# Attention and a two-product feed-forward in one kernel: float64 weight words put together from bytes, and three float32 head pairs scaled before their transposes

## Chip, cores and metric

The kernel runs on one core of a Trainium2 chip (trn2). The metric is the device time of one execution in microseconds, as a median over runs. Instructions run on five engines with queues of their own: TensorE (PE; its weight loads are listed as PEld), VectorE (DVE), ScalarE (ACT), GpSimd (POOL) and SyncE (SP), which here only issues DMAs.

## What is computed

Inputs: q, k and v, float32, 4 batches of 8 heads with 768 positions of 64 numbers; `moe_w_in` (512 x 2048) and `moe_w_out` (2048 x 512), float64.

```python
scores = q @ k.transpose(0, 1, 3, 2) / sqrt(64)
keep = (key < n_sink) | ((0 <= query - key) & (query - key < window))     # 4 sinks, window 128
scores = where(keep, scores, -1e9); scores -= scores.max(-1)
a = exp(scores); a = a / (a.sum(-1) + 1e-9)
x = (a @ v).transpose(0, 2, 1, 3).reshape(3072, 512)
h = x @ w_in
g = where(h >= 1, h, where(h <= -1, 0, (h + 1) ** 2 / 4))
out = g @ w_out
```

## The kernel before

**Chunks and units.** The 3072 tokens are worked on in 8 chunks of 384 (half a batch). A unit is one head of one chunk, so there are 64; chunk 0 needs units 0 to 7, and so on. The first 16 units (two chunks) are computed in float32, as 8 *pairs* of heads (`pair_load`, `pair_scores`, `pair_sums`, `early_transp`, `pair_r`, `pair_av`); the other 48 in split float32r (`load`, `scores`, `transp`, `av`, `sinks`).

**A float32 pair.** `pair_scores(m, i)` makes the scores of query tile i of both heads (TensorE, L441), adds the mask and takes the peak (VectorE, L452), and takes exponentials with their sums (ScalarE, L457). `pair_sums(m)` makes r = 1 / (sum + 1e-9), six numbers per partition (L464, L465). `early_transp` transposes p through PSUM (L474, L476) and ScalarE copies it back (L477 to L480). `pair_r(m)` spreads r over the head's 64 rows with six small products against the identity (L505) and copies the result to `xn` (ScalarE, L507). `pair_av(m)` multiplies the transposed p with v into PSUM (L493), and VectorE multiplies PSUM by what lies in `xn` (L496). Here r acts on the result, behind the products.

**Weights.** Each float64 matrix comes in as 32-bit word pairs. A *weight pair* n (16 of them) is 1 MB: two blocks of `w_in` (n even) or of `w_out` (n odd), 1024 numbers per partition, low and high word side by side, so a stream of high words has a step of 8 bytes. `decode_parts` makes a float32 of each and splits it: L170 shifts the high word left by 3 and masks it, L176 puts the two top bits back, L179 puts in the top three bits of the low word, ScalarE rounds to float32r (L180, `high`), VectorE subtracts (L183, `rest`). The three integer steps go through a tile `bits`. The first four weight pairs are decoded between the steps of the first pairs, in an order written out by hand (`first_pairs`, with `queue`, which chains instructions of one engine); the other twelve are spread among the steps of chunk 0's feed-forward, and each begins with `fetch`, which asks for the raw words of a few later ones. Raw and finished tiles share 8 buffers (`wpool`). The first four loads are issued on SyncE, the others on ScalarE's queue.

**Feed-forward.** Per chunk and per block j of 128 columns: `stage1` (12 matmuls, L588, three float32r products for one float32 one), the function g (L595 to L599), and `stage2` (9 matmuls, L607), two blocks behind. Chunk 0's GpSimd makes the low part `gl`, elsewhere VectorE does.

**What sets the order.** TensorE runs in program order. `spread` merges the steps of the next chunk's attention with those of this chunk's feed-forward by weights that stand beside each step; chunk 0 is merged with pairs 5 to 7, the end of pair 4 and units 16 and 17. On the other engines a scheduler with a timeline of its own sets the order, but for the instructions that are chained by `queue` or held by `keep_in_program_order`.

Of the kernel before, what the change touches and what calls it, by code (L numbers as in the profile page):

```python
# [20 lines left out]
NSINK = 4  # L21
KB = P + NSINK
# [27 lines left out]
def attn_ffn(ctx, tc, qk, qkp, vx, vs, par, w_in, w_out, out):  # L50
    nc = tc.nc
# [31 lines left out]
    low, high = par_f[:, :, 0], par_f[:, :, 1]  # L83
# [37 lines left out]
    behind = nc.gpsimd.memset(m1n[:, P:KB], 0.0).ins  # L121
# [7 lines left out]
    with tc.issue_after(behind):  # L129
# [4 lines left out]
        for r0 in (0, 32, 64, 96):  # L134
            t = tsel2[r0:r0 + R]
# [25 lines left out]
    with tc.issue_after(behind):  # L161
        nc.gpsimd.memset(both, -1)

    def decode_parts(t, w, words, pin=False, on=False):

        low, x = words[..., 0], words[..., 1]
        high, rest = (t[:, :, 0], t[:, :, 1]) if len(t.shape) == 4 else (t[:, 0], t[:, 1])

        def shift():
            first = nc.vector.tensor_scalar(w, x, 3, 0x3FFFFFFF, op0=ALU.logical_shift_left, op1=ALU.bitwise_and)  # L170
            if pin:
                tc.keep_in_program_order(first)
            queue(first, on)

        def sign():
            queue(nc.vector.scalar_tensor_tensor(w, x, -0x40000000, w, op0=ALU.bitwise_and, op1=ALU.bitwise_or), on)  # L176

        def tail():
            queue(nc.vector.scalar_tensor_tensor(w, low, 29, w, op0=ALU.logical_shift_right, op1=ALU.bitwise_or), on)  # L179
            queue(nc.scalar.copy(high, w.bitcast(F32)), on)  # L180

        def rest_of():
            queue(nc.vector.tensor_tensor(rest, w.bitcast(F32), high.bitcast(F32), op=ALU.subtract), on)  # L183

        return shift, sign, tail, rest_of

    def decode(t, w, words, pin=False):
        for f in decode_parts(t, w, words, pin):
            f()
# [4 lines left out]
    def weights(n):  # L194

        def src(k):
            return (w_in, w_out)[k % 2][k // 2 * 2:k // 2 * 2 + 2].bitcast(I32).rearrange("j p c -> p j c")

        def fetch():
            for k in range(n, min(n + min(AHEAD if n > 2 else 1, NP // 2 - n // 2 - 1) + 1, NP)):  # L200
                if k not in raw:
                    raw[k] = wpool.tile([P, 2, 2 * DM], I32, name="w")

                    with tc.issue_after(loaded[-1]) if k < SYNC else nullcontext():
                        (nc.sync if k < SYNC else nc.scalar).dma_start(raw[k], src(k))

        def parts(on):
            j, i = n // 2 * 2, n % 2
            words = raw[n].rearrange("p j (c two) -> p j c two", two=2)
            if i:  # L210
                t = wpool.tile([P, 2, 2, DM], F32R, name="w")
                w_o[j:j + 2] = t[:, 0], t[:, 1]
            else:
                t = wi2[n // 2]
            return decode_parts(t, dec.tile([P, 2, DM], I32, name=f"bits{n % 2}"), words, pin=not on, on=on)

        def f():
# [34 lines left out]
    st = {}  # L252
# [207 lines left out]
    def pair_sums(m):  # L460
        on = m < H // 2
        stat = st.pop(("sum", m))
        r = stat[:, :, CT:2 * CT]
        queue(nc.vector.tensor_scalar(r, stat[:, :, 0:CT], 1.0e-9, None, op0=ALU.add), on)  # L464
        queue(nc.vector.reciprocal(r, r), on)  # L465
        st["r", m] = r

    def early_transp(u, part):

# [12 lines left out]
    def pair_av(m):  # L482

        T = CT * P
        v_s = vq[m % 2]
        ps = ps_a.tile([P, 512], F32, name="ps_a")

        terms = [(2, 4, 1, 2), (0, 0, 2, 0), (1, 2, 2, 1), None]
        for n, t in enumerate(terms):
            for a in range(2):  # L490
                k, s0, ns, i = t or (CT, 0, 1, CT - 1)
                rhs = pt0[a][:, s0 * P:(s0 + ns) * P] if t else spn[a]
                nc.tensor.matmul(ps[a * D:a * D + D, i * P:(i + ns) * P], lhsT=v_s[:, k, a], rhs=rhs,  # L493
                                 start=(n == 0), stop=(n == len(terms) - 1))
        x = xn[:, units[2 * m][1] // 2, :]
        return lambda: queue(nc.vector.tensor_tensor(x, ps[:, :T], x, op=ALU.mult), m < H // 2)  # L496

    def pair_r(m):

        T = CT * P  # L500
        ps = ps_a.tile([P, 512], F32, name="ps_a")
        r = st.pop(("r", m))
        for i in range(CT):
            for a in range(2):
                nc.tensor.matmul(ps[a * D:a * D + D, i * P:(i + 1) * P], lhsT=r[:, a, i:i + 1].broadcast_to([P, D]),  # L505
                                 rhs=ident, start=True, stop=True)
        queue(nc.scalar.copy(xn[:, units[2 * m][1] // 2, :], ps[:, :T]), m < H // 2)  # L507

    def pair_steps(m):

        a, b = 2 * m - 2, 2 * m - 1
        sc = [(0.45, lambda i=i: pair_scores(m, i)) for i in range(CT)] if m < NATIVE // 2 else [(0.0, lambda: None)] * CT
        steps = [(0.0, lambda: pair_load(m + 1))] if m + 1 < NATIVE // 2 else []
        if m < NATIVE // 2:
            steps.append((0.0, lambda: pair_values(m)))
        tp = [(0.35, lambda u=u, i=i: early_transp(u, i)) for u in (a, b) for i in range(2)]
        pv = [(0.65, lambda: pair_r(m - 1)), (1.2, lambda: pair_av(m - 1)())]
        dg = [(0.0, lambda: pair_sums(m))] if m < NATIVE // 2 else []
# [143 lines left out]
    tail = []  # L662
# [159 lines left out]
```

## Time and profile before

| | us |
|---|---|
| median of three runs (705.91 to 710.62) | 706.29 |
| profiled execution | 705.98 |
| its span, from the first to the last instruction | 704.3 |
| TensorE busy in the span | 681.5 |
| VectorE busy | 510.3 |
| ScalarE busy | 489.5 |
| GpSimd busy | 278.8 |

A profile is of one execution. Busy time of TensorE is modelled, since matmuls overlap in its pipeline. A row of a group gives line, engine, operation, output and inputs with their shapes, how many, then busy time and the mean duration, then the engine's idle time just before them with what ended it. [...]

### The profile page before, as it was taken

Reading aid. Unit: us, or ns where it says so; the run is one execution under the profiler, and the core shown is the slowest. Engines: PE = TensorE matmul, PEld = TensorE weight load, DVE = VectorE, ACT = ScalarE, POOL = GpSimd, SP = SyncE. Lnnn points to the kernel's source line nnn. Section 1 sums busy time; section 2 is a strip of 40 time slices with the busy share of each in tenths; the row PEclk is TensorE's granted clock in tenths of the full one; section 3 lists DMA queues with packets and bytes.
Section 4 is the critical chain, followed back from the end, with each engine's and each line's share of the span. In section 5 each row is a group of like instructions: output and inputs, shape, how many; then the busy total and the mean of one; then the engine's idle time right before and its main releaser. Section 6 shows DMA issues by size and latency. Waiting matters only on the chain.

```text
span 704.3 us, 12263 instructions
## 1 busy us (share of the span) xinstructions
PE 681.5 (97%) x3889; PEld 604.6 (86%) x3889; DVE 510.3 (72%) x1405; ACT 489.5 (70%) x1241; POOL 278.8 (40%) x470
## 2 busy tenths in 40 slices
PE   5899998999999999999999999999999999999996
PEld 3567877899999999989889999899899999989995
DVE  7888998887776877688777878878787877642221
ACT  4886667687778868777787877777776876554332
POOL 3003344744443445355554455635544444300000
PEclk9899999999999999999999999999999999999999
DMA  7864533132244344254333443434322310001001
GB/s 232 291 216 156 190 99 135 49 107 60 63 148 124 102 127 129 68 174 128 92 113 105 147 130 124 126 118 133 122 59 62 102 50 22 3 1 45 1 1 49
DMA packets 45441, 73.98 MB, mean 105 GB/s; under 512 B 10744, under 2 KB 30008, under 8 KB 45368
## 3 DMA queue, kind: packets, MB, share of 16 engines
q1 hardware_dynamic: 42104, 60.53, 28.2%
q10 hardware_dynamic: 3264, 12.58, 4.8%
q8 instruction: 33, 0.54, 0.3%
q14 instruction: 40, 0.33, 0.1%
HBM read 66.80 MB, written 6.29 MB: 104 GB/s over the span
## 4 chain that ended last, share of the span: by engine, by line
PE 79%; DVE 9%; DMA 3%; ACT 3%; POOL 3%; issue 2%; SPq 0%; ACTq 0%; POOLq 0%; DVEq 0%
PE h_ps L588 33%; PE o_ps L607 32%; PE ps_a L283 4%; PE ps_a L390 4%; PE ps_a L344 2%; DVE bits L176 2%; DVE bits L179 1%; DMA w<-w_in 1%; POOL q_l L269 1%; PE ps_a L474 1%; DVE w L183 1%; DVE bits L170 1%; PE ps_a L493 1%; DVE p L304 1%; DVE g L597 1%
## 5 line engine op out<-in xcount | busy, mean ns | idle before, releaser
L588 PE MATMUL h_ps<-x,wi 128*128 128x384 f32 x1536 | 310.2, 340 | 0.0
L588 PEld LDWEIGHTS h_ps<-x,wi 128*128 128x128 f32 x1536 | 262.2, 188 | 8.7 <-issue 1.5
L607 PE MATMUL o_ps<-w,gh 128*128 128x512 f32 x768 | 244.0, 398 | 0.0
L607 PE MATMUL o_ps<-w,gl 128*128 128x512 f32 x384 | 151.1, 393 | 0.4 <-POOL gl L599 0.4
L607 PEld LDWEIGHTS o_ps<-w,gh 128*128 128x128 f32 x768 | 134.3, 188 | 16.9 <-issue 1.7
L597 DVE SCALAR_TENSOR_TENSOR g<-g,h_ps 128x384 f32<-128x384 f32 x128 | 70.3, 549 | 61.7 <-ACT g L596 60.6
L595 ACT ACTIVATE g<-h_ps,half 128x384 f32<-128x384 f32 x128 | 73.9, 578 | 52.7 <-PE h_ps L588 52.0
L269 POOL TENSOR_TENSOR q_l<-r,q_h 128x384 fp32r<-128x384 f32 x48 | 51.1, 1064 | 122.7 <-ACT q_h L268 116.1
L598 ACT CAST gh<-g 128x384 fp32r<-128x384 f32 x128 | 65.5, 512 | 46.1 <-DVE g L597 44.9
L290 ACT ACTIVATE p<-p,peak 128x260 f32<-128x260 f32 (+1 forms) x144 | 71.5, 496 | 23.0 <-DVE peak L287 22.4
L607 PEld LDWEIGHTS o_ps<-w,gl 128*128 128x128 f32 x384 | 72.0, 188 | 17.8 <-POOL gl L599 0.7
L599 DVE TENSOR_TENSOR gl<-g,gh 128x384 fp32r<-128x384 f32 x112 | 67.3, 601 | 23.5 <-ACT gh L598 22.6
L267 DVE TENSOR_TENSOR k_s<-k_r,k_s 64x524 fp32r<-64x524 f32 (+1 forms) x44 | 49.1, 1115 | 34.4 <-ACT k_s L265 34.3
L596 ACT ACTIVATE g<-g 128x384 f32<-128x384 f32 x128 | 67.0, 524 | 2.0
L287 DVE CUSTOM_DVE_ANT_0 p<-ps_a,m 128x260 f32<-128x260 f32 (+1 forms) x144 | 57.0, 407 | 14.7 <-PE ps_a L283 13.8
L358 POOL TENSOR_SCALAR_AFFINE_SELECT pt<-pt 128x384 fp32r<-128x384 f32 (+1 forms) x96 | 51.3, 535 | 22.6 <-DVE pt L349 19.5
L304 DVE CUSTOM_DVE_ANT_0 p<-p,stat 128x128 f32<-128x128 f32 x128 | 57.0, 489 | 0.2
L356 POOL TENSOR_SCALAR_AFFINE_SELECT pt<-pt 128x384 fp32r<-128x384 f32 (+1 forms) x96 | 49.9, 521 | 8.8 <-ACT pt L348 4.9
L599 POOL TENSOR_TENSOR gl<-g,gh 128x384 fp32r<-128x384 f32 x16 | 23.4, 1461 | 67.7 <-ACT gh L598 64.2
L390 PEld LDWEIGHTS ps_a<-pt,v_s 128*128 128x128 f32 x304 | 42.4, 190 | 1.8
L390 PE MATMUL ps_a<-pt,v_s 128*128 128x256 f32 (+1 forms) x304 | 41.9, 275 | 0.0
L283 PE MATMUL ps_a<-k_s,q_h 128*128 128x260 f32 (+1 forms) x144 | 40.7, 283 | 1.2 <-DVE sk L352 0.9
(151 smaller groups left out, 933.1 us busy)
## 6 DMA issues: line engine op xcount, KB each, us to landing
r<-qk SPq DMA_DIRECT2D x48, 192.0 KB
k_r<-qk SPq DMA_DIRECT2D x32, 262.0 KB
again<-w_in SPq DMA_DIRECT2D x16, 512.0 KB
again<-w_out SPq DMA_DIRECT2D x16, 512.0 KB
w<-w_in ACTq DMA_DIRECT2D x6, 1024.0 KB
w<-w_out ACTq DMA_DIRECT2D x6, 1024.0 KB
out<-o SPq DMA_DIRECT2D x23, 256.0 KB
r<-vx SPq DMA_DIRECT2D x32, 128.0 KB
```

Source lines behind the costliest of these rows:

```text
L269: nc.gpsimd.tensor_tensor(q_l, q_r, q_h.bitcast(F32), op=ALU.subtract)
L283: nc.tensor.matmul(ps[:, lo:260], lhsT=q[:, i * P:(i + 1) * P], rhs=k_s[:, c0:c0 + 260 - lo], start=(j == 0), stop=(j == len(qs) - 1))
L290: nc.scalar.activation(p[:, i, lo:260], p[:, i, lo:260], AF.Exp, bias=peak_i, scale=-1.0, accum_out=stat[:, i:i + 1])
L304: nc.vector.tensor_tensor_reduce(out=own, in0=own, in1=p[:, i, 0:P], scale=r, scalar=0.0, op0=ALU.add, op1=ALU.add, accum_out=stat[:, i:i ...
L390: nc.tensor.matmul(z, lhsT=w, rhs=y, start=(n == 0), stop=(n == len(mms) - 1))
L588: nc.tensor.matmul(h_ps[:, :T], lhsT=w_i[j][:, w, ct * P:(ct + 1) * P], rhs=x[:, y, ct], start=(ct == 0 and n == 0), stop=(ct == NCT - 1 a ...
L595: nc.scalar.activation(g, h_ps[:, :T], AF.Relu, bias=half, scale=0.5)
L596: nc.scalar.activation(g, g, AF.Square)
L597: nc.vector.scalar_tensor_tensor(g, g, 1.0, h_ps[:, :T], op0=ALU.min, op1=ALU.max)
L598: nc.scalar.copy(gh, g)
L599: (nc.gpsimd if row0 == GL_POOL else nc.vector).tensor_tensor(gl, g, gh.bitcast(F32), op=ALU.subtract)
L607: nc.tensor.matmul(o_ps[tt], lhsT=gg[:, tt * P:(tt + 1) * P], rhs=w_o[j][:, w], start=(j == 0 and n == 0), stop=(j == NJ - 1 and n == 2))
```

## The change

Four things change.

1. A weight word is made in one step from the high word and a tile `ends` (128 x 1024 words, set to 0 once by GpSimd). Two VectorE instructions write single bytes into `ends`: byte 0 of each word gets the top three bits of the low word, byte 3 gets the sign and the bits that turn the exponent. Then `word` shifts the high word left by 3 and takes the xor with `ends`. The result goes over the low words of the raw pair (for the last weight pair into `ends`), so the cast and the subtraction read it from there, with a step of 8 bytes. The tiles `bits` are gone.
2. The raw pair is now in use until the subtraction. `fetch` looks one pair less ahead in places: pair 13 is asked for by step 12 instead of step 11, pair 14 behind the decode of pair 13 instead of ahead of it, pair 15 behind the decode of pair 14.
3. Pairs 5 to 7 (`SCALED`): right behind the sums VectorE multiplies the six tiles of p by r, in place. `pair_r` falls away for them, and `pair_av` ends with a copy by ScalarE instead of VectorE's product.
4. `pair_steps` orders the steps differently: scores and sums of pair m stand ahead of the last transposes of pair m - 1, and the product with v comes last.

The old decode lives on in the code for inputs out of the fast path's range, which isn't run here.

```diff
+SCALED = range(5, NATIVE // 2)
...
+    def decode_parts(t, ends, words, w, on):
+        x = words[..., 1]
+        b = words.bitcast(U8).rearrange("p j c (w e) -> p j c w e", e=4)
+        e = ends.rearrange("p j c -> p (j c)").bitcast(U8).rearrange("p (j c e) -> p j c e", j=2, e=4)
...
+        def put(i):
+            if not on:
+                tc.keep_in_program_order(i)
+            queue(i, on)
...
         def tail():
-            queue(nc.vector.scalar_tensor_tensor(w, low, 29, w, op0=ALU.logical_shift_right, op1=ALU.bitwise_or), on)
+            put(nc.vector.tensor_scalar(e[..., 0], b[..., 0, 3], 5, 0x07, op0=ALU.logical_shift_right,
+                                        op1=ALU.bitwise_and))
         def sign():
-            queue(nc.vector.scalar_tensor_tensor(w, x, -0x40000000, w, op0=ALU.bitwise_and, op1=ALU.bitwise_or), on)
+            put(nc.vector.tensor_scalar(e[..., 3], b[..., 1, 3], 0x80, 0xC0, op0=ALU.bitwise_and, op1=ALU.bitwise_xor))
+        def word():
+            queue(nc.vector.scalar_tensor_tensor(w, x, 3, ends, op0=ALU.logical_shift_left, op1=ALU.bitwise_xor), on)
             queue(nc.scalar.copy(high, w.bitcast(F32)), on)
...
-            for k in range(n, min(n + min(AHEAD if n > 2 else 1, NP // 2 - n // 2 - 1) + 1, NP)):
+            for k in range(n, min(n + min(AHEAD if n > 2 else 1, max(NP // 2 - 1 - (n + 1) // 2, 0)) + 1, NP)):
...
-            return decode_parts(t, dec.tile([P, 2, DM], I32, name=f"bits{n % 2}"), words, pin=not on, on=on)
+            return decode_parts(t, ends, words, ends if n == NP - 1 else words[..., 0], on)
...
+            if NP - 4 < n < NP - 1:
+                wsteps[n + 1].load()
...
+        if m in SCALED:
+            for a in range(2):
+                for i in range(CT):
+                    p = early_p(2 * m + a)[:, i, KB if i == 0 else 0:260]
+                    nc.vector.tensor_scalar(p, p, r[:, a, i:i + 1], None, op0=ALU.mult)
...
+        if m in SCALED:
+            return lambda: nc.scalar.copy(x, ps[:, :T])
...
-        pv = [(0.65, lambda: pair_r(m - 1)), (1.2, lambda: pair_av(m - 1)())]
+        pv = [(1.2, lambda: pair_av(m - 1)())]
+        if m - 1 not in SCALED:
+            pv = [(0.65, lambda: pair_r(m - 1))] + pv
...
-        return steps + tp[:1] + sc[:1] + tp[1:] + sc[1:2] + pv + sc[2:] + dg
+        if m == 5:
+            return steps + tp[:1] + sc[:1] + tp[1:] + sc[1:2] + pv[:1] + sc[2:] + dg + pv[1:]
+        return steps + tp[:1] + sc[:1] + tp[1:2] + sc[1:2] + tp[2:3] + sc[2:] + dg + tp[3:] + pv
```

On VectorE, at the sums of pair 5, in the kernel before (`stat` holds sums and r; `bits_806` is weight pair 7):

```order
L464 TENSOR_SCALAR stat<-stat 128x2x3
L465 RECIPROCAL stat<-stat 128x2x3
L170 TENSOR_SCALAR bits_806<-w 128x1024
L176 SCALAR_TENSOR_TENSOR bits_806<-w,bits_806 128x1024
L597 SCALAR_TENSOR_TENSOR g<-g,h_ps 128x384
L179 SCALAR_TENSOR_TENSOR bits_806<-w,bits_806 128x1024
```

And in the changed one (L188 and L192 write the bytes, L195 the word, L199 subtracts, L488 scales):

```order
L188 TENSOR_SCALAR ends<-w 128x1024
L192 TENSOR_SCALAR ends<-w 128x1024
L199 TENSOR_TENSOR wi_158<-w,wi_158 128x2x512
L479 TENSOR_SCALAR stat<-stat 128x2x3
L195 SCALAR_TENSOR_TENSOR w<-w,ends 128x1024
L480 RECIPROCAL stat<-stat 128x2x3
L488 TENSOR_SCALAR pt<-pt,stat 128x128
L488 TENSOR_SCALAR pt<-pt,stat 128x260 x2
L488 TENSOR_SCALAR pt<-pt,stat 128x128
L488 TENSOR_SCALAR pt<-pt,stat 128x260 x2
L627 SCALAR_TENSOR_TENSOR g<-g,h_ps 128x384
```

A decode has two one-source instructions and one with two sources ahead of its cast, and the bytes of weight pair 7 stand ahead of the subtraction of pair 6; the scaling follows the reciprocal at once. Between the third scores of pairs 5, 6 and 7 and their first transposes, TensorE's order has 18 or 21 `h_ps` matmuls and three to five groups of three `o_ps` matmuls.

On ScalarE, the load of weight pair 14 in the kernel before (`wi6` is the cast of weight pair 12, `w_1200` the raw pair 14; the cast of weight pair 13 comes 13 rows after the first):

```order
L180 CAST wi6_161<-bits0_1139 128x2x512
L205 DMA w_1200<-w_in 128x2x1024
L457 ACTIVATE pt_188,stat_1011<-pt_188,peak_97 128x260
L596 ACTIVATE g_1166<-g_1166 128x384
L480 COPY pt_187<-ps_a_1179 128x384
```

And in the changed one (`w_1139` is the raw pair 13, `w_1197` pair 14):

```order
L196 CAST w_1191<-w_1139 128x2x512
L626 ACTIVATE g_1213<-g_1213 128x384
L501 COPY pt_190<-ps_a_1224 128x256
L502 COPY spn1_180<-ps_a_1224 4x128
L217 DMA w_1197<-w_in 128x2x1024
L628 CAST gh_1214<-g_1213 128x384
```

The load moved from behind the cast of pair 12 to behind that of pair 13 and three more instructions.

On VectorE, where the changed kernel takes up weight pair 14 (the first rows are of pair 13, the second L188 of pair 14):

```order
L188 TENSOR_SCALAR ends<-w 128x1024
L192 TENSOR_SCALAR ends<-w 128x1024
L199 TENSOR_TENSOR wi_161<-w,wi_161 128x2x512
L195 SCALAR_TENSOR_TENSOR w<-w,ends 128x1024
L199 TENSOR_TENSOR w<-w 128x2x512
L627 SCALAR_TENSOR_TENSOR g<-g,h_ps 128x384 x2
L188 TENSOR_SCALAR ends<-w 128x1024
L192 TENSOR_SCALAR ends<-w 128x1024
L302 ISA p,peak<-ps_a,m_109 128x128
```

The same place before (`bits_1203` is weight pair 13, `bits_1271` pair 14):

```order
L179 SCALAR_TENSOR_TENSOR bits_1203<-w,bits_1203 128x1024
L597 SCALAR_TENSOR_TENSOR g<-g,h_ps 128x384
L183 TENSOR_TENSOR w<-bits_1203,w 128x2x512
L496 TENSOR_TENSOR xn<-ps_a,xn 128x384
L170 TENSOR_SCALAR bits_1271<-w 128x1024
L176 SCALAR_TENSOR_TENSOR bits_1271<-w,bits_1271 128x1024
```

Pair 14 still follows pair 13 closely, while its load now follows pair 13's cast; the first scores of unit 16 (L302, before L287) stand right behind it.

## Rows read from the trace of the kernel before

**Rows 1.** The page's busy time of the engines.

```profile
PE 681.5 (97%) x3889; PEld 604.6 (86%) x3889; DVE 510.3 (72%) x1405; ACT 489.5 (70%) x1241; POOL 278.8 (40%) x470
```

**Rows 2.** Windows by stage: busy time of PE, PEld, DVE, ACT, POOL; clock, DMA.

```profile
12.90:44.70 31.80, 24.69 (x203) 17.10 (x202) 29.36 (x85) 25.49 (x84) 0.91 (x2) 0.89 0.79 264
44.70:123.80 79.10, 76.94 (x472) 61.46 (x471) 70.16 (x120) 52.83 (x134) 30.22 (x22) 1.00 0.43 148
...
136.00:650.00 514.00, 512.84 (x2893) 468.22 (x2892) 379.59 (x1123) 378.14 (x957) 232.88 (x403) 1.00 0.31 96
```

**Rows 3.** Chain of waits by line, 12.9 to 44.7, then 44.7 to 123.8.

```profile
by line: DVE bits L179 10.9%; PE ps_a L474 9.8%; DVE bits L176 7.4%; DVE pt L452 6.8%; ACT wi L180 6.6%; ACT pt L457 6.3%; PE ps_a L493 5.0%; PE h_ps L588 4.5%; DVE bits L170 4.3%; DVE p L452 4.2%; DVE x L619 3.9%; DVE w L183 3.8%; ACT p L4
...
by line: PE h_ps L588 21.8%; PE o_ps L607 13.9%; DVE bits L176 9.5%; DVE bits L179 7.1%; issue 4.8%; DVE w L183 4.4%; DVE wi L183 3.8%; PE ps_a L493 3.7%; DVE bits L170 3.4%; DVE g L597 3.2%; PE ps_a L441 3.0%; PE ps_a L474 2.9%; PE ps_a L5
```

**Rows 4.** Groups of VectorE's instructions, 0 to 140 us.

```profile
L179 DVE SCALAR_TENSOR_TENSOR bits<-w,bits 128x1024 int32<-128x1024 int32 x16 | 22.2, 1389 | 0.2
L176 DVE SCALAR_TENSOR_TENSOR bits<-w,bits 128x1024 int32<-128x1024 int32 x16 | 21.8, 1365 | 0.3
L170 DVE TENSOR_SCALAR bits<-w 128x1024 int32<-128x1024 int32 x16 | 11.4, 711 | 2.9 <-DMA w<-w_in 2.9
L183 DVE TENSOR_TENSOR wi<-bits,wi 128x1024 fp32r<-128x1024 f32 x8 | 10.6, 1326 | 4.4 <-ACT wi L180 4.4
L183 DVE TENSOR_TENSOR w<-bits,w 128x1024 fp32r<-128x1024 f32 x8 | 9.8, 1223 | 2.4 <-ACT w L180 2.4
L597 DVE SCALAR_TENSOR_TENSOR g<-g,h_ps 128x384 f32<-128x384 f32 x16 | 8.7, 544 | 0.0
...
L496 DVE TENSOR_TENSOR xn<-ps_a,xn 128x384 f32<-128x384 f32 x8 | 4.4, 551 | 0.4 <-PE ps_a L493 0.3
```

**Rows 5.** VectorE with a pointer scalar: line L302, then a group.

```profile
L302 DVE TENSOR_SCALAR p<-p,stat x16: 275/283/1049, 122.5 to 267.0; 128x128 f32<-128x128 f32 x16
...
L114 DVE TENSOR_SCALAR m<-x,nw 128x260 f32<-128x260 f32 x1 | 0.3, 350 | 0.0
```

**Rows 6.** Lines L170 and L176: ns min/median/max, first and last start.

```profile
L170 DVE TENSOR_SCALAR bits<-w x16: 650/682/1046, 12.9 to 123.8; 128x1024 int32<-128x1024 int32 x16
L176 DVE SCALAR_TENSOR_TENSOR bits<-w,bits x16: 1210/1225/2074, 13.6 to 124.9; 128x1024 int32<-128x1024 int32 x16
```

**Rows 7.** ScalarE: line L239, then groups, 0 to 140 us.

```profile
L239 ACT COPY top<-again x32: 637/658/672, 196.7 to 508.7; 128x512 uint8<-128x512 uint8 x32
...
L180 ACT CAST wi<-bits 128x1024 fp32r<-128x1024 f32 x8 | 8.4, 1047 | 6.5 <-DVE bits L179 6.5
L596 ACT ACTIVATE g<-g 128x384 f32<-128x384 f32 x16 | 8.3, 520 | 0.2
L477 ACT COPY pt<-ps_a 128x256 f32<-128x256 f32 x16 | 5.9, 366 | 1.3 <-PE ps_a L476 1.2
```

**Rows 8.** Chain of waits in order of time: start us, us, what.

```profile
4.95 7.92 DMA w<-w_in
...
149.57 2.08 PE h_ps L588 x12
```

**Rows 9.** Instructions in order of time: start us, us, engine, line.

```profile
72.01 0.88 PE L505 MATMUL ps_a<-ident,stat 128*64 128x128 f32 x12
...
117.20 0.38 ACTq L205 DMA_DIRECT2D w<-w_out  x1
...
122.89 0.87 PE L344 MATMUL ps_a<-ident,p 128*128 128x128 f32 x3 [1.94 <-DVE p L302]
...
123.76 0.68 DVE L170 TENSOR_SCALAR bits<-w 128x1024 int32<-128x1024 int32 x1
```

**Rows 10.** Windows of 1 us as in rows 2; the last column is GB/s.

```profile
118.00:119.00 1.00, 1.00 (x9) 1.00 (x8) 0.62 (x3) 1.00 (x6) 0.00 (x0) 1.00 0.08 33
...
121.00:122.00 1.00, 0.00 (x0) 0.00 (x0) 0.00 (x0) 1.00 (x5) 0.91 (x2) 1.00 0.61 223
```

**Rows 11.** Groups of GpSimd's instructions, 0 to 12.9 us.

```profile
L162 POOL MEMSET both<- 128x256 int32 x1 | 0.3, 312 | 0.1
```

More of the change, by code (lines that the diff above doesn't have):

```diff
@@ L162, in attn_ffn, with decode, tail @@
         nc.gpsimd.memset(both, -1)
-    def decode_parts(t, w, words, pin=False, on=False):
+    def decode(t, w, words):
         low, x = words[..., 0], words[..., 1]
         high, rest = (t[:, :, 0], t[:, :, 1]) if len(t.shape) == 4 else (t[:, 0], t[:, 1])
[L169 to L173, printed above, removed]
+        nc.vector.tensor_scalar(w, x, 3, 0x3FFFFFFF, op0=ALU.logical_shift_left, op1=ALU.bitwise_and)
+        nc.vector.scalar_tensor_tensor(w, x, -0x40000000, w, op0=ALU.bitwise_and, op1=ALU.bitwise_or)
+        nc.vector.scalar_tensor_tensor(w, low, 29, w, op0=ALU.logical_shift_right, op1=ALU.bitwise_or)
+        nc.scalar.copy(high, w.bitcast(F32))
+        nc.vector.tensor_tensor(rest, w.bitcast(F32), high.bitcast(F32), op=ALU.subtract)
+    def decode_parts(t, ends, words, w, on):
+        x = words[..., 1]
+        b = words.bitcast(U8).rearrange("p j c (w e) -> p j c w e", e=4)
+        e = ends.rearrange("p j c -> p (j c)").bitcast(U8).rearrange("p (j c e) -> p j c e", j=2, e=4)
+        high, rest = t[:, :, 0], t[:, :, 1]
+        def put(i):
+            if not on:
+                tc.keep_in_program_order(i)
+            queue(i, on)
+        def tail():
+            put(nc.vector.tensor_scalar(e[..., 0], b[..., 0, 3], 5, 0x07, op0=ALU.logical_shift_right,
+                                        op1=ALU.bitwise_and))
         def sign():
-            queue(nc.vector.scalar_tensor_tensor(w, x, -0x40000000, w, op0=ALU.bitwise_and, op1=ALU.bitwise_or), on)
-        def tail():
-            queue(nc.vector.scalar_tensor_tensor(w, low, 29, w, op0=ALU.logical_shift_right, op1=ALU.bitwise_or), on)
+            put(nc.vector.tensor_scalar(e[..., 3], b[..., 1, 3], 0x80, 0xC0, op0=ALU.bitwise_and, op1=ALU.bitwise_xor))
+        def word():
+            queue(nc.vector.scalar_tensor_tensor(w, x, 3, ends, op0=ALU.logical_shift_left, op1=ALU.bitwise_xor), on)
             queue(nc.scalar.copy(high, w.bitcast(F32)), on)
@@ L183, in rest_of @@
             queue(nc.vector.tensor_tensor(rest, w.bitcast(F32), high.bitcast(F32), op=ALU.subtract), on)
[L185 to L189, printed above, removed]
+        return tail, sign, word, rest_of
     top = {}
@@ L220, in f @@
                 g()
+            if NP - 4 < n < NP - 1:
+                wsteps[n + 1].load()
+        f.load = fetch
         if n < WFIRST:
@@ L464, in pair_sums @@
         queue(nc.vector.tensor_scalar(r, stat[:, :, 0:CT], 1.0e-9, None, op0=ALU.add), on)
-        queue(nc.vector.reciprocal(r, r), on)
-        st["r", m] = r
+        last = nc.vector.reciprocal(r, r)
+        if not on:
+            tc.keep_in_program_order(last)
+        queue(last, on)
+        if m in SCALED:
[3 more added lines that the diff above has]
+                    nc.vector.tensor_scalar(p, p, r[:, a, i:i + 1], None, op0=ALU.mult)
+        else:
+            st["r", m] = r
     def early_transp(u, part):
@@ L516, in pair_steps @@
         tp = [(0.35, lambda u=u, i=i: early_transp(u, i)) for u in (a, b) for i in range(2)]
-        pv = [(0.65, lambda: pair_r(m - 1)), (1.2, lambda: pair_av(m - 1)())]
+        pv = [(1.2, lambda: pair_av(m - 1)())]
+        if m - 1 not in SCALED:
+            pv = [(0.65, lambda: pair_r(m - 1))] + pv
         dg = [(0.0, lambda: pair_sums(m))] if m < NATIVE // 2 else []
-        if m % (H // 2) == 0:
-            return steps + tp[:3] + sc[:1] + tp[3:] + pv[:1] + sc[1:2] + pv[1:] + sc[2:] + dg
-        return steps + tp[:1] + sc[:1] + tp[1:] + sc[1:2] + pv + sc[2:] + dg
+        if m == NATIVE // 2:
+            return steps + tp[:3] + sc[:1] + tp[3:] + pv + sc[1:] + dg
+        if m == 5:
+            return steps + tp[:1] + sc[:1] + tp[1:] + sc[1:2] + pv[:1] + sc[2:] + dg + pv[1:]
+        return steps + tp[:1] + sc[:1] + tp[1:2] + sc[1:2] + tp[2:3] + sc[2:] + dg + tp[3:] + pv
     def first_pairs():
@@ L654, in attn_ffn @@
     spn = [dec.tile([P, P], F32, name=f"spn{i}") for i in range(2)]
+    ends = dec.tile([P, 2, DM], I32, name="ends")
+    with tc.issue_after(behind):
+        nc.gpsimd.memset(ends, 0)
     for t in vq + spn:
```

## The prediction

> **What bounds the kernel now.** I read the page's busy times first, then busy time by stage, then the chain of waits inside each early stage, then the groups of VectorE's instructions there. The page has TensorE busy for 97% of the span [rows 1], but matmuls are pipelined, so that says little about the first stages. By stage [rows 2] the reader is to see that VectorE (DVE) is busy for 29.36 of 31.80 us while the first four weight pairs are decoded (12.9 to 44.7) and for 70.16 of 79.10 us while the other twelve are (44.7 to 123.8). From 136 to 650 us TensorE has 512.84 of 514.00, and VectorE 379.59: there nothing on VectorE can move the end. So the change, which acts before 136 us, is worth what it does to the time at which that full stretch begins.
>
> The chain in the two early stages [rows 3] is shared. In the first, `bits L179` has 10.9% and `bits L176` 7.4%, and the rest is spread over all engines; in the second TensorE's two big products have 35.7% and the decode lines L170, L176, L179 and L183 together 28.2%. VectorE and TensorE bound this stage in turns, so an instruction on VectorE counts for the part of it that lies on the chain. L176 has 0.074 x 31.8 = 2.4 us and 0.095 x 79.1 = 7.5 us there, 9.9 of its 21.8 us of busy time [rows 4]: 45%. With the order kept, shortening an instruction can't save more than its part on the chain, and lengthening one can't cost less; I take 40 to 45% for everything on VectorE.
>
> **Decode (16 times).** Before: one one-source instruction (L170, mean 0.711 us), three with two sources (L176 1.365, L179 1.389, L183 about 1.275) [rows 4]. After: two one-source byte instructions, one xor with two sources, the same subtraction. So L176 goes and a second one-source instruction comes. No row shows VectorE on bytes. [...] L170 is the nearest row: 1024 elements read at a step of 8 bytes, one source, 0.682 us median [rows 6], about half of L176, whose source has the same step. I take L170's mean. Per decode 2 x 0.711 - 0.711 - 1.365 = -0.654 us, 16 times -10.5 us of VectorE. On the chain: L176's 9.9 us shrink to 0.711/1.365 of themselves, **-4.7 us**.
>
> [...]
>
> The xor writes into the raw pair at a step of 8 bytes, and the cast and the subtraction read it so. Reading so costs nothing on VectorE: L176 reads at that step in 1.225 us, and L183 reads contiguous words in a mean of 1.223 [rows 4, 6]. ScalarE: 512 bytes at an 8-byte step take 0.658 us (L239) and 1024 contiguous words 1.047 (L180) [rows 7]; at worst 2 x 0.658 - 1.047 = +0.27 us a cast, on an engine busy for 52.83 of 79.10 us; I take 0. No row has VectorE writing at that step: between 0 and 2.074 - 1.225 = +0.85 us (L176's slowest [rows 6]); I take 0, the nearest row being the read.
>
> [...]
>
> **Scaling pairs 5 to 7.** Each adds six one-source instructions with a pointer scalar: two of 128 elements (L302, 0.283) and four of 260 (L114, 0.350) [rows 5], 1.97 us, and drops L496 on VectorE (0.551 [rows 4]): +1.41 a pair, +4.2 us in all, at 40% **+1.7 us** (0 to 4.2). The wait that it adds (transposes now need the scaled p, not the exponentials alone) is hidden: in the order shown the scaling stands right behind the sums, and between a pair's last scores and its first transposes TensorE has at least 18 h_ps products, 3.1 us at 12 in 2.08 [rows 8], and three o_ps groups. Without that cover, up to 2 us a pair. ScalarE swaps one copy for another: 0.
>
> TensorE loses 12 matmul records a pair at L505, 0.88 us from 72.01 [rows 9], 2.6 us for three. TensorE is busy for 76.94 of 79.10 us there, but part of that is waiting under the pipeline: between 0 and -2.6, I take **-1.5 us**; it includes the PSUM bank that these no longer hold.
>
> **Loads.** Pair 13 is asked for one step later, and pair 14 only behind the cast of pair 13. In the order shown ScalarE has three more instructions ahead of that DMA, so it is issued about 1.05 + 1.1 us after the xor of pair 13 has ended (cast L180 1.05, then 0.52 and 0.37 for a square and a copy, L596 and L477 [rows 7], and a copy of 4 rows that I put at 0.2). A load issued at 117.20 [rows 9] moves its bytes from 118 to before 122 [rows 10], 4.5 us; the first load was on the chain for 7.92 [rows 8]. So pair 14 is there about 6.7 us after that xor. VectorE has ahead of it only the wait for the cast (1.05), the subtraction (1.22) and two writes of g (L597, 0.54 each [rows 4]): 3.4 us. It stands still for about 3.3 us, where before the last pair started at 123.76 without a wait [rows 9]. Behind the waiting byte instruction stand the second one and the first masked scores of the next attention (L287), on which TensorE's transposes wait already (1.94 us at 122.89 [rows 9]). I take **+2.5 us**, since TensorE has some products ready; the ends are 0 and, with the first load's 7.92, 2.1 + 7.9 - 3.4 = 6.6. Before that the loads are ahead by a step or more: 0. Pair 15 has longer: 0.
>
> The memset of `ends` on GpSimd (1024 words; 256 take 0.31 us [rows 11]) lies before the first load lands, for which VectorE waits 2.9 us till 12.9 [rows 4, 6]: 0.
>
> **Sum:** -4.7 + 1.7 - 1.5 + 2.5 = -2.0 us. The profiled execution took 705.98 us (span 704.3 and 1.7 around it), 0.3 under the median of 706.29 of the three runs. 705.98 - 2.0 = **704.0 us**.
>
> **Rivals.**
> 1. *VectorE is the only bound, and all that it sheds counts.* For it: 92% and 89% busy in the two stages. Against it: TensorE's 35.7% of the chain. -10.5 + 4.2 - 2.6 = -8.9, with the late load lost in the gain: 697.
> 2. [...] Place: the two byte instructions of every decode; price 1.225 us each: 16 x (2 x 1.225 - 2.076) = +6.0 us, and VectorE, with +10.2 us in all, is busy nearly throughout, so that 40 to 100% of it counts: 705.98 + 2.5 - 1.5 + (4.1 to 10.2) = 711 to 717, say 714. It decides from 1.04 us a byte instruction on (half of 0.711 + 1.365), where the decode gains nothing. For it: no row of bytes. Against it: L170's rate.
> 3. *The xor's write at 8-byte steps is slow.* 15 x 0.85 = 12.7 us at 45% is +5.7: 704.0 + 5.7 = 710. Against it: the reads.
> 4. *The late load takes as long as the first one did:* 6.6 in place of 2.5 us, 708. Against it: far fewer bytes are moved by then [rows 2].
>
> **How the numbers follow.** Forecast 55% (its own range 700 to 707), rival 1 17%, rival 2 12%, rival 3 10%, rival 4 6%. A measurement of this kernel can tell about 1%, 7 us, from no change. Faster than 699.2: nearly all of rival 1 and a tenth of the forecast, 0.22. Slower than 713.4: most of rival 2 and a little of 3, 0.13. The rest 0.65. The range leaves out the lowest part of rival 1 and the upper half of rival 2: 696.5 to 713.5.
>
> **What would show it.** Right: byte instructions near 0.7 us; the xor near 1.23; VectorE's busy time before 136 us some 6 us less; VectorE idle for 2 to 4 us ahead of the byte instruction of pair 14, released by a DMA; the last decode some 3 us earlier. Wrong: byte instructions over 1 us (rival 2); the xor over 1.6 (rival 3); an early stage that ends 8 us sooner with TensorE still busy (rival 1); transposes of pairs 5 to 7 that wait for the scaling by over 1 us, which none of my cases holds.

## The result, and the profile after

The changed kernel took 710.90 us, the median of 13 runs (708.24 to 715.17), beside 706.02 us of the kernel before in the same comparison (13 runs, 703.05 to 710.62). The ratio is 1.0065, with a 95% interval of 1.0045 to 1.0086: slower by 4.6 us (0.0065 x 706; 3.2 to 6.1). The forecast was 2.0 us faster. The time lies inside the stated range and within 1% of before, but the sign was wrong, and the sum missed by 6.6 us. That the range holds is luck: it reaches up to there for slow byte instructions and a slow xor (rivals 2 and 3), which did not come.

The profiled execution has a span of 708.3 us, 4.0 over that of before. The page's busy time, which answers to [rows 1]:

```profile
PE 677.3 (96%) x3853; PEld 602.3 (85%) x3853; DVE 505.1 (71%) x1420; ACT 490.7 (69%) x1241; POOL 276.8 (39%) x471
```

VectorE is busy for 5.2 us less and TensorE for 4.2 us less, in a longer time. The windows by stage, columns as in [rows 2]:

```profile
12.90:44.70 31.80, 23.39 (x206) 16.23 (x205) 26.47 (x82) 26.21 (x85) 0.91 (x2) 0.95 0.82 278
44.70:123.80 79.10, 72.94 (x427) 58.91 (x426) 63.72 (x123) 50.69 (x120) 26.00 (x19) 1.00 0.37 125
136.00:650.00 514.00, 511.62 (x2887) 467.21 (x2886) 382.78 (x1125) 378.89 (x961) 232.18 (x404) 1.00 0.31 96
```

From 136 us on TensorE is nearly full in both; it is busy there for 1.2 us less than before, which the forecast did not have. The larger part lies ahead of that. Between 44.7 and 123.8 us VectorE is busy for 63.72 us where it was 70.16, and TensorE, which was busy for 76.94, for 72.94: it now stands idle for 6.2 us where it was 2.2. So the question is what TensorE waits for. The chain that ended last, followed back, doesn't lead through this stage in the changed kernel, so there is no row to set beside [rows 3], and the waits are read instead. The waits by engine, TensorE's, 44.7 to 123.8 us (line, whom it waited for, us in total, times, longest), of the kernel before and then of the changed one:

```profile
PE ps_a L344 <- DVE p L302: 1.9, 1, 1.9
PE ps_a L474 <- ACT pt L480: 0.2, 1, 0.2
```

```profile
PE ps_a L517 <- ACT pt L501: 3.4, 2, 2.0
PE ps_a L498 <- DVE pt L488: 2.6, 1, 2.6
```

The wait of 1.9 us is still there (L359 for L317), only later, at 126 us. New are 2.6 us at the first transposes of pair 5, for the scaling (L488), and 3.4 us at the values products of pairs 5 and 7 (L517), for the copies of the last transposes (L501). Together 6.0 us, and they stand at the scaling, whose wait the forecast called hidden, and at the new order of the steps, for which its sum has no term.

**The parts of the decode.** VectorE's groups, 0 to 140 us, which answer to [rows 4]:

```profile
L195 DVE SCALAR_TENSOR_TENSOR w<-w,ends 128x1024 int32<-128x1024 int32 x15 | 21.3, 1423 | 0.1
L192 DVE TENSOR_SCALAR ends<-w 128x1024 uint8<-128x1024 uint8 x16 | 12.2, 764 | 0.0
L188 DVE TENSOR_SCALAR ends<-w 128x1024 uint8<-128x1024 uint8 x16 | 12.2, 762 | 2.6 <-POOL ends L687 1.4 <-DMA w<-w_out 1.3
L199 DVE TENSOR_TENSOR wi<-w,wi 128x1024 fp32r<-128x1024 f32 x8 | 10.9, 1363 | 3.5 <-ACT wi L196 3.5
L199 DVE TENSOR_TENSOR w<-w 128x1024 fp32r<-128x1024 f32 x7 | 9.1, 1305 | 5.0 <-ACT w L196 5.0
```

A byte instruction takes 0.76 us, 0.05 more than the 0.711 that was taken, L170's mean for as many words. The xor's mean is 1.42 us, near the two instructions of [rows 4]; its minimum and median are in the line's own view, with those of the cast (L196) and the scaling (L488), in ns:

```profile
L195 DVE SCALAR_TENSOR_TENSOR w<-w,ends x15: 1210/1226/2030, 13.7 to 121.2; 128x1024 int32<-128x1024 int32 x15
...
L196 ACT CAST w<-w x7: 1107/1122/1161, 23.8 to 111.9; 128x1024 fp32r<-128x1024 f32 x7
...
L488 DVE TENSOR_SCALAR pt<-pt,stat x12: 280/348/1049, 65.2 to 104.1; 128x260 f32<-128x260 f32 x8, 128x128 f32<-128x128 f32 x4
```

1.226 us for 1024 words read and written at a step of 8 bytes is L176's 1.225 [rows 6]. The cast pays 0.08 us for its step (1.122 against 1.047 [rows 7]).

### The profile page after: what moved, and what is told of

Read it like the earlier page. It is cut to its first block, busy times and chain, and to the rows that moved or that the text cites. A ratio compares the mean times of both kernels' runs of the same rounds, so it can differ in the third digit from the quotient of the medians.

```text
span 708.3 us, 12215 instructions
## 1 busy us (share of the span) xinstructions
PE 677.3 (96%) x3853; PEld 602.3 (85%) x3853; DVE 505.1 (71%) x1420; ACT 490.7 (69%) x1241; POOL 276.8 (39%) x471
## 5 line engine op out<-in xcount | busy, mean ns | idle before, releaser
L302 DVE CUSTOM_DVE_ANT_0 p<-ps_a,m 128x260 f32<-128x260 f32 (+1 forms) x144 | 57.2, 408 | 14.6 <-PE ps_a L298 13.8
L373 POOL TENSOR_SCALAR_AFFINE_SELECT pt<-pt 128x384 fp32r<-128x384 f32 (+1 forms) x96 | 49.9, 521 | 21.6 <-DVE pt L364 18.6
L371 POOL TENSOR_SCALAR_AFFINE_SELECT pt<-pt 128x384 fp32r<-128x384 f32 (+1 forms) x96 | 49.6, 518 | 8.3 <-ACT pt L363 4.3
```

The costliest lines, as they stand in the source:

```text
L302: nc.vector.tensor_tensor_reduce(out=p[:, i, lo:260], in0=ps[:, lo:260], in1=m, scale=-0.125, scalar=3.0e38, op0=ALU.add, op1=ALU.min, acc ...
```

## How TensorE comes to wait for the scaling

The instructions in order of time at the first of the new waits:

```profile
59.30 0.42 DVE L467 CUSTOM_DVE_ANT_0 pt<-ps_a,m 128x260 f32<-128x260 f32 x1
...
60.58 0.77 DVE L188 TENSOR_SCALAR ends<-w 128x1024 uint8<-128x1024 uint8 x1
...
61.24 0.75 DVE L192 TENSOR_SCALAR ends<-w 128x1024 uint8<-128x1024 uint8 x1
61.54 1.28 POOL L629 TENSOR_TENSOR gl<-g,gh 128x384 fp32r<-128x384 f32 x1 [3.25 <-ACT gh L628]
61.87 2.04 DVE L199 TENSOR_TENSOR wi<-w,wi 128x1024 fp32r<-128x1024 f32 x1
...
63.90 1.21 DVE L195 SCALAR_TENSOR_TENSOR w<-w,ends 128x1024 int32<-128x1024 int32 x1
65.03 0.18 DVE L480 RECIPROCAL stat<-stat 128x6 f32<-128x6 f32 x1
...
65.25 1.54 DVE L488 TENSOR_SCALAR pt<-pt,stat 128x128 f32<-128x128 f32 x6
65.59 0.47 PEld L498 LDWEIGHTS ps_a<-ident,pt 128*128 128x128 f32 x3 [2.93 <-DVE pt L488]
65.59 0.70 PE L498 MATMUL ps_a<-ident,pt 128*128 128x128 f32 x3 [2.61 <-DVE pt L488]
```

The last mask of pair 5 is issued on VectorE at 59.30, and the scaling at 65.25. Between them stands a decode: two bytes, a subtraction, an xor. The subtraction takes 2.04 us in place of its median of 1.23, while GpSimd makes a `gl` from 61.54 to 62.82. The other two subtractions over 1.3 us, 1.81 us from 98.84 and 1.53 from 124.25, also began while GpSimd was at work (`q_l` from 98.56 to 99.57, `k_s` from 123.67 to 124.71); that of 56.22 took 1.20 us beside a `gl` of 2.08 from 56.21. That GpSimd's instruction holds up VectorE's is a reading of the three slow rows; no run parts the two. TensorE has products until 63.0 and then nothing. The prediction counted the cover on TensorE (3.1 us and some o_ps groups) and that "the scaling stands right behind the sums", but not what stands ahead of the sums in VectorE's queue, although the order listed for the changed kernel showed these very instructions.

The waits of 3.4 us have the same form on ScalarE. The larger one is at the values product of pair 7 (L517). Last transposes (L500), cast of a weight pair (L196), copy of the transposes (L501) and product in the changed kernel, and then, with the same `o_ps` groups between transposes and product, in e8 (below):

```profile
109.74 0.27 PE L500 MATMUL ps_a<-ident,pt 128*4 128x128 f32 x1
111.33 0.43 PE L517 MATMUL ps_a<-pt,vq 128*64 128x128 f32 x2
111.94 1.11 ACT L196 CAST w<-w 128x1024 fp32r<-128x1024 f32 x1 [1.69 <-issue]
113.38 0.35 ACT L501 COPY pt<-ps_a 128x256 f32<-128x256 f32 x1
113.78 1.29 PE L517 MATMUL ps_a<-pt,vq 128*64 128x128 f32 x10 [2.01 <-ACT pt L501]
```

```profile
108.16 0.27 PE L500 MATMUL ps_a<-ident,pt 128*4 128x128 f32 x1
109.21 0.36 ACT L501 COPY pt<-ps_a 128x256 f32<-128x256 f32 x1
109.76 1.30 PE L517 MATMUL ps_a<-pt,vq 128*64 128x128 f32 x12
110.75 1.14 ACT L196 CAST w<-w 128x1024 fp32r<-128x1024 f32 x1 [1.04 <-DVE w L195]
```

Where the copy stands behind the cast, TensorE waits for 2.0 us; where it stands ahead, TensorE doesn't wait.

## Experiments

All comparisons are with runs of the kernel before on the same chip in the same set. Microseconds below are (ratio - 1) x 706.

**First set: which part costs.** Two things were undone one at a time and together: the scaling (`SCALED = range(0)`) and the order in `pair_steps` (its two old return lines). A fourth kernel has these two alone, on the old decode with its loads.

e1, neither scaling nor new order: the decode and its loads alone.

> Theory A (the new decode saves some 3 us as forecast, and the steps of pairs 5 to 7 lose it: with the scaling inside VectorE's queue and with the last transposes right ahead of the values product, TensorE waits 2.6 + 1.4 + 2.0 us that it did not wait before): with the scaling and the new order of the steps both undone, 702 to 704 us, and TensorE's waits at the pairs' transposes and values products of 62 to 112 us are back to under 0.5 us each. Theory B (the new decode itself costs: loads later, ScalarE's cast at an 8-byte step, DMA issues in ScalarE's queue behind waits): 709 to 711 us, as the changed kernel.

705.79 us, ratio 1.0000 (0.9986 to 1.0014). Neither theory: the decode is worth 0, not -3. VectorE's instructions in order of time show the late load:

```profile
110.81 0.56 DVE L522 TENSOR_TENSOR xn<-ps_a,xn 128x384 f32<-128x384 f32 x1 [1.11 <-PE ps_a L517]
114.21 0.78 DVE L188 TENSOR_SCALAR ends<-w 128x1024 uint8<-128x1024 uint8 x1 [2.85 <-DMA w<-w_in]
```

e2, scaling with the old order.

> The changed kernel with the scaling kept and the order of the steps of pairs 5 to 7 as before. Theory A, with the order as the larger part: 705 to 707 us, the waits of 1.4 and 2.0 us at the values products gone, the wait for the scaling (2.6 us) still there or longer, because the transposes stand no later than before. Theory A, with the scaling as the larger part: 708 to 710. Theory B: 709 to 711.

721.81 us, ratio 1.0219 (1.0199 to 1.0239), +15.5 us: far worse than either expectation. The waits of TensorE, 44.7 to 123.8 us:

```profile
PE ps_a L498 <- DVE pt L488: 6.3, 3, 3.5
PE ps_a L498 <- DVE p L488: 3.9, 2, 3.7
```

e3, new order without scaling.

> The changed kernel without the scaling (the last three pairs take the reciprocal through TensorE again), with the new order of the steps. Theory A, with the order as the larger part: 707 to 710 us, waits of over 1 us at the values products still there and the wait for VectorE at the first transposes under 1 us. Theory A, with the scaling as the larger part: 703 to 706. Theory B: 709 to 711.

710.31 us, ratio 1.0064 (1.0043 to 1.0085), +4.5: as much as the whole change, though most of it isn't lost in pairs 5 to 7 (see the positions below). Its waits are not at the values products, as was expected, but at copies (1.6 us) and at unit 16's scores:

```profile
PE ps_a L298 <- DVE peak L302: 2.6, 1, 2.6
PE ps_a L498 <- ACT pt L504: 1.6, 2, 1.2
```

Ahead of those scores VectorE stood still for weight pair 14:

```profile
117.71 0.76 DVE L188 TENSOR_SCALAR ends<-w 128x1024 uint8<-128x1024 uint8 x1 [3.94 <-DMA w<-w_in]
```

e4, old decode with the scaling and the new order.

> The kernel before with the scaling and the new order of the steps alone, decode and loads as they were. Theory A: 709 to 714 us, slower than the changed kernel, because VectorE's queue is longer in front of the scaling. Theory B: 703 to 706 us, as the kernel before or a little faster.

714.42 us, ratio 1.0111 (1.0091 to 1.0132), +7.8, 0.4 us above theory A's range. So on top of the new steps the new decode takes off 3.2 us (7.8 - 4.6), while on top of the old ones it gave nothing (e1). The wait for the scaling is 5.1 us in this profile: with the old decode VectorE's queue ahead of it is longer. From the last mask of pair 5 to the scaling it is 9.0 us here (59.07 to 68.04) and 6.0 in the changed kernel.

**Second set: the late load.** In e5 to e7 the xor writes to a tile of its own, the raw pair is free at the xor, and `fetch` is that of the kernel before:

```diff
-            for k in range(n, min(n + min(AHEAD if n > 2 else 1, max(NP // 2 - 1 - (n + 1) // 2, 0)) + 1, NP)):
+            for k in range(n, min(n + min(AHEAD if n > 2 else 1, NP // 2 - n // 2 - 1) + 1, NP)):
...
-            return decode_parts(t, ends, words, ends if n == NP - 1 else words[..., 0], on)
+            return decode_parts(t, ends, words, bits, on)
...
-            if NP - 4 < n < NP - 1:
-                wsteps[n + 1].load()
...
+    bits = dec.tile([P, 2, DM], I32, name="bits")
```

e5 is e1 with this, e6 the changed kernel with it, e7 is e3 with it.

> The decode alone as in e1, but the xor writes its words to a tile of their own, contiguous, so that the raw pair is free at the xor and loads are asked for as in the kernel before. Theory A2 (the decode gains 2 to 3 us of path, and the late load of weight pair 14, for which VectorE waited 2.8 us in e1, takes them back): 702.5 to 704 us, VectorE's wait for that load under 0.5 us. Theory B2 (the gain of VectorE is off the path in any case, TensorE sets the end): 705 to 706.5 us, as e1, with the wait gone.

> The changed kernel with the same separate tile and loads. Theory A2, applied to the whole change: its waits lie at the pairs' transposes and values products, not at a load (VectorE waited 1.3 us for a load in the profile), so it gains about 1 us: 709 to 711 us. Rival (the weight loads in ScalarE's queue, late behind the subtraction, hold up ScalarE's copies and so the values products): 705 to 707 us.

> The new order of the steps without the scaling, with the separate tile and loads. If the late load (3.9 us of VectorE's waiting in e3, and 2.6 us of TensorE's for the masked scores behind it) makes the new order's cost, 705 to 707.5 us; if the order itself does, 709 to 711.

| us against before | raw pair holds the words | tile of their own |
|---|---|---|
| old order, no scaling | 0.0 (e1) | -2.7 (e5: 704.11, 0.9962, 0.9948 to 0.9976) |
| new order, no scaling | +4.5 (e3) | -0.2 (e7: 706.33, 0.9997, 0.9983 to 1.0010) |
| new order and scaling | +4.6 (the change) | +1.5 (e6: 707.81, 1.0021, 1.0007 to 1.0034) |
| old order and scaling | +15.5 (e2) | not run |

Keeping the words in the raw pair costs 2.7 us in the first row, 4.7 in the second and 3.1 in the third. That is the price of the late loads together with the casts' 0.08 us each at a step of 8 bytes; the two were not parted. For e5 theory A2 held in substance: its 704.11 stands 0.1 above the stated range, and VectorE has no wait for a load any more. e7's result is the one expected of the late load: with the raw pair free, the new order is level with the kernel before. Beside e5 it still costs 2.5 us. For e6 the two expectations left out what came: 3.1 us of gain, though its profile still has 4.0 us of waits at the values products:

```profile
PE ps_a L514 <- ACT pt L498: 4.0, 2, 2.0
```

What is gone there is the wait for the scaling. On VectorE the sums and the scaling of pair 5 now stand ahead of the bytes of weight pair 7 (60.22 and 62.95 us), 2.2 us behind the last mask, and TensorE's first transposes begin at 62.31 without a wait. With 9.0, 6.0 and 2.2 us from mask to scaling, TensorE waits for 5.1 us (e4), 2.6 (the change) and not at all (e6): with the same steps on TensorE, the wait follows the queue ahead of the scaling. What made the order on VectorE another in e6 is not known.

e8, the changed kernel with the last scores between the last transposes and the values product, as cover for the copy. The line that it edits is used for the values products of pairs 5 and 6; that of pair 7 has a line of its own, which stays:

```diff
-        return steps + tp[:1] + sc[:1] + tp[1:2] + sc[1:2] + tp[2:3] + sc[2:] + dg + tp[3:] + pv
+        return steps + tp[:1] + sc[:1] + tp[1:2] + sc[1:2] + tp[2:] + sc[2:] + dg + pv
```

> The changed kernel with the last scores of the next pair moved between the last transposes of a pair and its values product (pairs 6 and 7), as cover for ScalarE's copy. If the bare copy ahead of the values products is what costs (1.4 and 2.0 us), 707 to 709 us with those waits under 0.5 us; if not, or if the wait moves to the scaling, 710 to 714.

716.81 us, ratio 1.0138 (1.0117 to 1.0160), +9.7, above both ranges. The values products wait no more, that of pair 7 with the copy ahead of the cast on ScalarE (shown above), and TensorE still waits 2.6 us for the scaling. But the time isn't lost in the pairs: behind the last of them TensorE is 0.5 us ahead of the kernel before. It is lost later, at unit 16's scores (a wait of 3.2 us, behind VectorE's wait of 2.4 us for the load of weight pair 14) and at the products with the last weight pair (1.6 us for its cast and 2.4 for its subtraction, at 137 and 140 us). The granted clock, 1.00 from 44.7 to 106 us, is 0.94 from 106 to 123.8 and 0.92 from there to 140. So the pairs lose less than in the change, and what comes behind them takes more than that. How much of it is due to the late loads is open: e8 with early loads was not run.

**Third set: where the decode's gain counts.** e9 has e5's decode for the first four weight pairs and the old three-step decode for the rest, e10 the other way round; e11 is e5 with the memset of `ends` ahead of GpSimd's other work.

> e5 with the new decode for the first four weight pairs alone (up to 44.7 us), the decode of before for the other twelve. Theory A3 (an instruction saved on VectorE counts only where TensorE stands idle: nearly in full in the first stage, not in the second, where TensorE is busy for 97% and only 2 us can be gained): 703.5 to 704.5 us, the same as e5 within 0.7 us. Theory B3 (45% of every decode lies on the path, as forecast): a quarter of e5's gain is left, 705.5 to 706.5 us.

> e5 with the new decode for the last twelve pairs alone, the decode of before for the first four. Theory A3: 706 to 707 us, as the kernel before within 0.7 us, though VectorE is busy for some 7 us less between 44.7 and 124 us. Theory B3: three quarters of e5's gain, 704 to 705 us.

> e5 with the memset of ends on GpSimd moved from 10.3 us to about 2 us, so that the first byte instruction waits for its load alone. If the memset held up the first decode in most executions (by up to 1.4 us in the profile of the changed kernel), 702.8 to 703.6 us; if the load lands after 11.3 us in most of them, as in the profiles of before, e1 and e3 (11.9 to 12.9), 704 us as e5.

| | median us | ratio | interval |
|---|---|---|---|
| e9, first four new | 705.48 | 0.9999 | 0.9984 to 1.0014 |
| e10, last twelve new | 704.17 | 0.9970 | 0.9959 to 0.9982 |
| e11, ends early | 703.88 | 0.9962 | 0.9947 to 0.9978 |

Theory A3 fell. The gain lies with the last twelve decodes (-2.1 us), and the first four give nothing that can be measured, although VectorE is busy for 92% of their stage. Theory B3's quarter, 0.7 us, lies within the interval too, so e9 doesn't exclude it. The windows of 44.7 to 123.8 us, of e10:

```profile
44.70:123.80 79.10, 77.45 (x479) 62.49 (x477) 64.74 (x126) 54.30 (x139) 27.02 (x22) 1.00 0.43 148
```

VectorE is busy for 64.74 us there, 5.4 less than before, and TensorE for 77.45, 0.5 more. What of A3 stands is its upper bound: TensorE's idle time in that stage was 2.2 us before [rows 2], and no more than that could come back. Why the first stage gives nothing was not settled. e11 equals e5: the memset was not what held it up.

**e12, the scaling's work without its wait.** e1 with the eighteen scaling instructions writing to a spare tile:

```diff
...
+                    nc.vector.tensor_scalar(spare[:, KB if i == 0 else 0:260], p, r[:, a, i:i + 1], None, op0=ALU.mult)
```

> e1 (new decode, steps in the order of before) with the eighteen scaling instructions of e2 as work alone: they write to a spare tile, nobody waits for them, and the last three pairs take the reciprocal through TensorE as before. If the scaling costs by VectorE's time (5.9 us, of which the decode runs count about a quarter), 706 to 708 us; if it costs by the wait that it puts in front of the transposes, as e2's 10.2 us of TensorE's waits say, 706 to 708 too but far from e2's 721.8, with no wait of TensorE for the scaling. 715 or more would say that VectorE's work is what e2 paid for.

710.23 us, ratio 1.0055 (1.0034 to 1.0075), +3.9: above the 706 to 708 that were expected, and far from e2's 15.5. In e12 TensorE has no wait for the scaling; the waits are at unit 16, 2.3 us for its masks (L303) and 3.1 for its weights p (L318). Ahead of the masks VectorE waited 1.7 us for the late load of weight pair 14, and the granted clock is 0.50 from 124 to 130 us. So the 3.9 us aren't the price of the eighteen instructions by themselves; what they cost with early loads was not run.

**Where each kernel loses its time.** The start of TensorE's last `h_ps` product of a block of the feed-forward, read from the trace of each profiled execution, less that of the kernel before, in us. Blocks are counted from 0. Up to block 4 of chunk 0 no wait for the scaling has come; block 12 stands behind the values product of pair 7; block 5 of chunk 1 stands behind unit 16 and the last weight pair.

| | block 4 | block 12 | chunk 1, block 5 |
|---|---|---|---|
| before, from the span's start | 64.4 | 113.7 | 161.8 |
| the change | -1.7 | +3.6 | +3.0 |
| e1, decode alone | -1.7 | -2.1 | -0.9 |
| e2, scaling, old order | -0.8 | +15.0 | +15.4 |
| e3, new order, no scaling | -1.4 | 0.0 | +3.5 |
| e5, decode alone, early loads | -2.3 | -2.8 | -2.5 |
| e6, the change, early loads | -2.2 | +2.3 | +1.1 |
| e7, new order, early loads | -2.1 | -2.0 | -1.3 |
| e8, scores between | -2.2 | -0.5 | +8.7 |
| e12, scaling's work alone | -1.2 | -0.2 | +4.1 |

From block 4 to block 12, in the steps of pairs 5 to 7, the change falls back by 5.3 us (differences are taken before rounding). The new order without the scaling falls back by 1.4 (e3) or 0.2 (e7), and the scaling's work without its wait by 1.0 (e12). e3 and e12 lose most of their time later, at unit 16, where their load of weight pair 14 is late; the change loses nothing more there, and e2 0.4.

## Why the prediction was wrong

| step | forecast | measured, us | from | or | from |
|---|---|---|---|---|---|
| new decode, without its loads | -4.7 | -2.7 | e5 | -2.7 | e5 |
| late load of pair 14 | +2.5 | +2.7 | e1 less e5 | +3.1 | change less e6 |
| new order of the steps | 0 | +4.5 | e3 less e1 | +2.5 | e7 less e5 |
| scaling and the products that it drops | +1.7 - 1.5 | +0.1 | change less e3 | +1.7 | e6 less e7 |
| sum | -2.0 | +4.6 | | +4.6 | |

Each difference of two ratios is uncertain by about 1.5 us (two intervals of some 1 us either way). The parts depend on one another, so the table has two ways through them: with the late loads put in first, and with them put in last. That the scaling costs 0.1 us by the first way is an accident of it: e3 loses its time at unit 16, where the change, later by then, loses none. The -1.5 us for the dropped products, with what it has in it for a PSUM bank, was the author's estimate from L505's 0.88 us a pair; no run shows it apart from the scaling.

**The step that failed** is the cover of the scaling, and with it the order of the steps. The prediction said of the wait that the scaling adds that it "is hidden", and its sum has no term at all for the fourth edit, the new order. In the change TensorE waits 2.6 us for the scaling and 3.4 us for the copies ahead of two values products, and falls back by 5.3 us in these steps, which turns a lead of 1.7 us into 3.6 us of delay. The two edits go together. Without a new order the scaling costs 15.5 us (e2), with 10.2 us of TensorE's waits for it at five places; the new order takes these down to one of 2.6 us, and adds those at the copies. The prediction counted what TensorE has to do between a pair's scores and its transposes, and not what VectorE has to do ahead of the scaling, nor ScalarE ahead of the copy. It named the sign in its last part, transposes of pairs 5 to 7 that wait for the scaling by over 1 us, "which none of my cases holds"; it should have been a case. "Without that cover, up to 2 us a pair" was too low as well: e2 has 10.2 us for three pairs.

**The decode** was right in its instructions and mis-sized on the path. VectorE's busy time fell by 5.2 us in the span; the forecast for decode and scaling was 6.3. But 45% of the decode's 10.5 us, the share of time that L176 has on the chain, gave -4.7, and the runs give 26% (2.7 of 10.5). The chain says who came last, not by how much: TensorE's products stand right behind and are the chain as soon as VectorE is faster. In the second stage the row with TensorE busy for 76.94 of 79.10 us [rows 2] was the tighter bound: 2.2 us idle, beside a gain of 2.1 there (e10). The prediction had that row.

**The late load** was right in place, mechanism and size in e1 to e3: VectorE stood still for 2.85, 3.6 and 3.94 us (forecast 3.3), with the bytes and unit 16's masked scores queued behind. In the changed kernel's own profile the wait isn't there: VectorE stood still then for a product instead,

```profile
118.92 0.56 DVE L627 SCALAR_TENSOR_TENSOR g<-g,h_ps 128x384 f32<-128x384 f32 x1 [4.15 <-ACT g L626]
```

because TensorE had waited 2.0 us at a values product just before. One delay covered the other. Why early loads still gave 3.1 us to the change (e6) is seen only in part: the wait for the scaling is gone, but TensorE falls back by 4.5 us in the pairs where the change falls back by 5.3, and the rest is spread ahead of them and behind.

**The rivals.** Byte instructions of 1.225 us (2) and a slow xor (3) fell by the rows above, with 0.76 us and a median of 1.226. No cost of the xor's write at a step of 8 bytes is seen: in e5, writing contiguous words, it took 1.224 us. VectorE as the only bound (1) fell with e5: the decode alone, with early loads, gave 2.7 us, while VectorE was busy for 9.3 us less (501.0 against 510.3). Rival 4, a load as slow as the first one, would have kept VectorE waiting for longer than these 2.85 to 3.94 us. The memset of `ends` was put at nothing since a load was later; in the profile of the change it was not (VectorE waited 1.4 us for it), in the runs it made no difference (e11).

**A version that beats both** is e5: the byte decode with words in a tile of their own, early loads, no scaling, old order. It took 704.11 us, ratio 0.9962 to the kernel before, which is 0.4% less; e11 has the same ratio.

## What to carry to other kernels

An added dependency is priced by two queues: what stands ahead of its producer on that engine (9.0, 6.0 and 2.2 us in e4, the change and e6), and what the consumer's engine has to do meanwhile (e2's old order has no steps of the pair before between sums and transposes; there pairs 6 and 7 wait up to 3.7 and 2.6 us, in the change not at all). A wait on one path can also hide a wait on another, so undoing edits one at a time can put a cost down to the wrong one; look where in the trace each variant falls back. A share of a chain of waits is an upper bound for a gain; hold it against the idle time of the engine that comes next in the same stage, and take the smaller. A result that is written over its own input keeps that buffer in use for longer: look up which load waits for the buffer before the saved tile counts as free.

## What was not expected of the hardware

The granted clock of TensorE fell in and behind some of the waits. The windows of e2 around its wait of 3.7 us, which ended at 92.03 (columns as before; the clock is the third number from the end):

```profile
86.00:88.00 2.00, 2.00 (x11) 1.58 (x9) 1.65 (x5) 1.01 (x1) 0.00 (x0) 1.00 0.00 0
88.00:90.00 2.00, 0.34 (x2) 0.00 (x0) 1.23 (x1) 2.00 (x7) 1.34 (x1) 1.00 0.00 0
90.00:92.00 2.00, 0.00 (x0) 0.00 (x0) 1.49 (x4) 0.82 (x3) 1.24 (x2) 0.84 0.70 176
92.00:94.00 2.00, 1.77 (x7) 0.98 (x7) 2.00 (x5) 0.99 (x2) 0.99 (x1) 0.50 1.01 408
94.00:96.00 2.00, 2.00 (x7) 1.69 (x6) 2.00 (x9) 0.12 (x1) 0.00 (x0) 0.50 0.41 147
96.00:98.00 2.00, 2.00 (x9) 1.82 (x8) 1.20 (x3) 0.76 (x4) 0.00 (x0) 0.50 0.01 4
98.00:100.00 2.00, 2.00 (x13) 1.82 (x12) 0.15 (x1) 1.74 (x4) 0.00 (x0) 0.95 0.00 0
```

1.00 is full speed and 0.50 half of it. TensorE begins 11 to 13 matmuls in 2 us before and after, and 7 to 9 at 0.50. The clock stands at 0.50 from 92 to 98 us, so up to 3 us of work were lost behind the wait of 3.7 us (an estimate: half of these 6 us). In the second stage of e2 the mean granted clock is 0.89; in the changed kernel, with waits of 2.6, 1.4 and 2.0 us, it stayed at 1.00. In e12, with waits of 2.3 and 3.1 us that ended at 122.09 and 126.39, it is 0.50 from 124 to 130 us. By the estimate the wait of 3.7 us cost more than its own length, which is part of why e2 is so far out.
